# Attention, then two MoE layers: U = v_m w_in formed one head at a time in 64 by 32 tiles

## The chip, the cores and the metric

One core of a Trainium2 chip runs the whole program. The metric is the device time of one execution in microseconds (us); lower is better.

## The reference

Three layers run one after the other. Attention over a small memory comes first: for each of 8 batches and 8 heads, 576 rows of `k` and `v` are gathered into 32 memory rows.

```python
a   = softmax(phi, axis=2)                      # b h s m, m = 32
k_m = einsum('bhsm,bhsd->bhmd', a, k)           # normalised by the sum over m
v_m = einsum('bhsm,bhsd->bhmd', a, v)           # 32 x 64 for each batch and head
attn = softmax(q @ k_m.T / 8)                   # b h s m
x = (attn @ v_m) laid out as 4608 x 512
x = relu(x @ w_in) ** 2 @ w_out                 # 512 -> 2048 -> 512
logits = x @ w_gate; e = argmax(logits)         # 8 experts, each 512 -> 1024 -> 512
out = gate * relu(x @ w1[e]) @ w2[e]
```

The inputs come in double precision; the kernel reads them as pairs of 32-bit words.

## The kernel before

The kernel never forms `attn @ v_m`. It folds `v_m` into `w_in`: for each batch b, `U = v_m w_in` has one row for each (head, memory row), 256 rows, and 2048 columns, and the hidden layer is `attn U`. The 8 heads are two groups g of four heads; the 128 rows of a group fill the 128 partitions of a bank.

Stage one makes tokens in 12 blocks of 384 (`NB`), and each block in 16 steps f (`NF`), n counting all 192 steps. `g1(n)` (L638) multiplies `attnT` with a slice of U (L650, six matmuls for each batch in the block), ScalarE squares the result (L658 to L661), VectorE takes the remainder (L662), and `g2` (L675, matmuls at L670) accumulates the second layer. Between these steps the main loop puts in pieces of three generators: `attention(b)` for the next batch, `weight_stream()` (L577), which loads the experts' weights, splits them in two halves of 16 bits and stores them, and `route()` (L711) for finished blocks. Stage two, from about 840 us on, runs the experts over 39 tiles (`e1_mm`, `e2_mm`). In stage one a planner, which runs when the kernel is built, fixes the order of the instructions on each engine out of the program's order, priorities and dependencies.

Inside `attention(b)`, `s_kv` makes `k_m` and `v_m` in four column tiles of 32 (L366) and writes each head's 64 columns twice, next to each other, into `kvn` (L385). `s_tr(g)` (L390) transposes them, so that the 64 dimensions lie in partitions 0 to 63 and again in 64 to 127. A `mask` (L399) then zeroes, in each pair of heads, the half that belongs to the other head; the result is `vbd`. `s_scale` (L402) splits `vbd` into two halves of 16 bits, `v16`, for batches from `UB` = 3 on. `u_steps(b)` (L539) makes U: for each of four chunks of 512 columns (ch) and each g, one bank of `side_bank` (L95, three banks, shared with every other small product) is filled by two column tiles of 64 (x), each a matmul with all 128 rows, half of which multiply zeros. Batches 0 to 2 do that in fp32 (L554; every fp32 matmul runs as two instructions), batches 3 to 7 in three fp16 products (L563). ScalarE then writes the high half of U (L569) and VectorE the low half (L570). Each (ch, g) is one step of the generator; the loop takes one to three steps for each n.

`w_in` is loaded in 16 jobs of 128 rows by `load_next` (L208, DMA at L215) on SyncE's queue, through a ring of four places (`RAWS`). Job n holds rows `128 (n % 4)` on, that is two heads, and chunk `n // 4`. `conv` (L224) turns each into fp32. The 16 jobs of `w_out` follow through the same ring.

## Time and profile before

| | |
|---|---|
| median of 3 runs | 1335.16 us (1334.47 to 1335.77) |
| the profiled execution | 1334.69 us |
| its span, first to last instruction | 1332.6 us |
| TensorE matmul busy | 1173.5 us, 88% |
| VectorE, ScalarE busy | 676.7 us, 661.2 us |
| mean granted clock of TensorE | 0.958 of 2.4 GHz |

PE is TensorE's matmul, PEld its weight load, DVE VectorE, ACT ScalarE, SP SyncE with its queue of DMAs. The PE's busy time is the union of its matmuls' times from start to modelled end; two matmuls that follow each other overlap by the length of the array's pipeline, so the distance from start to start says more than one duration. U shows up under the tile name `u` (the bank) and `U` (the result).

### The profile page before, as it was taken

Reading aid. Unit: us, or ns where it says so; the run is one execution under the profiler, and the core shown is the slowest. Engines: PE = TensorE matmul, PEld = TensorE weight load, DVE = VectorE, ACT = ScalarE, POOL = GpSimd, SP = SyncE. Lnnn points to the kernel's source line nnn. Section 1 sums busy time; section 2 is a strip of 40 time slices with the busy share of each in tenths; the row PEclk is TensorE's granted clock in tenths of the full one; section 3 lists DMA queues with packets and bytes.
Section 4 is the critical chain, followed back from the end, with each engine's and each line's share of the span. In section 5 each row is a group of like instructions: output and inputs, shape, how many; then the busy total and the mean of one; then the engine's idle time right before and its main releaser. Section 6 shows DMA issues by size and latency. Waiting matters only on the chain.

```text
span 1332.6 us, 21300 instructions
## 1 busy us (share of the span) xinstructions
PE 1173.5 (88%) x7146; PEld 597.4 (45%) x7146; DVE 676.7 (51%) x1644; ACT 661.2 (50%) x1347; POOL 113.9 (9%) x169
## 2 busy tenths in 40 slices
PE   1538989998988998898999999998998998879896
PEld 1214546444545544455555465543443443334342
DVE  5798987877886885786546543342110111101100
ACT  2467877797875877685666665521111111111111
POOL 2000000101010101000000100013000000000000
PEclk9558999998989999898999999999999999999998
DMA  6957659468749469536040110476558457695762
GB/s 168 261 190 207 189 137 265 158 213 260 216 163 266 154 213 287 159 132 150 24 103 10 40 25 24 126 169 167 97 120 181 104 123 193 151 227 118 151 159 61
DMA packets 264369, 205.23 MB, mean 154 GB/s; under 512 B 209855, under 2 KB 228287, under 8 KB 264256
## 3 DMA queue, kind: packets, MB, share of 16 engines
q1 hardware_dynamic: 257616, 182.67, 53.7%
q0 software_dynamic: 6640, 21.16, 4.6%
q8 instruction: 58, 0.95, 0.3%
q14 instruction: 55, 0.45, 0.1%
HBM read 234.53 MB, written 55.76 MB: 218 GB/s over the span
## 4 chain that ended last, share of the span: by engine, by line
issue 33%; PE 24%; DMA 17%; DVE 13%; ACT 6%; POOL 4%; SPq 2%; POOLq 0%; ACTq 0%; DVEq 0%
PE acc L670 12%; DMA wstage<-in_moe_w_dram 6%; PE h L650 6%; POOL out_dram L92 3%; DMA scr<-rec,sl 2%; DMA e_t<-in_phi_dram 2%; DVE wo L629 2%; ACT wo L628 1%; DMA ws<-wo 1%; PE u L563 1%; DMA raw_ring<-in_moe_w_out_dram 1%; DVE g L662 1%; DMA raw_ring<-in_moe_w_in_dram 1%; ACT wo L601 1%; DVE wm L180 1%
## 5 line engine op out<-in xcount | busy, mean ns | idle before, releaser
L670 PE MATMUL acc<-wo,g 128*128 128x512 f16 x1728 | 421.1, 383 | 16.5 <-DVE g L662 9.9
L670 PEld LDWEIGHTS <-g 128*128 128x128 f16 x1728 | 166.0, 99 | 197.5 <-issue 22.1
L650 PE MATMUL h<-attnT,U 128*128 128x384 f16 (+1 forms) x1536 | 233.5, 290 | 13.8 <-ACT U L569 9.8
L1001 PE MATMUL e<-w2t,gT 128*128 128x512 f16 x936 | 211.5, 381 | 22.3 <-DMA gT<-g 14.6
L974 PE MATMUL e<-w1t,xT 128*128 128x512 f16 x936 | 211.2, 381 | 11.4 <-DMA w1t<-ws 8.0
L986 DVE SCALAR_TENSOR_TENSOR g<-e,g 128x512 f16<-128x512 f32 x78 | 50.3, 686 | 297.5 <-ACT g L985 297.3
L650 PEld LDWEIGHTS <-U 128*128 128x128 f16 x1536 | 140.1, 99 | 104.2 <-issue 26.6
L1001 PEld LDWEIGHTS <-gT 128*128 128x128 f16 x936 | 91.2, 98 | 137.4 <-DMA gT<-g 18.5
L974 PEld LDWEIGHTS <-xT 128*128 128x128 f16 x936 | 91.5, 98 | 124.9 <-issue 13.7
L662 DVE TENSOR_TENSOR g<-r,g 128x384 f16<-128x384 f32 x192 | 105.6, 553 | 78.3 <-ACT r L661 77.8
L658 ACT ACTIVATE r<-h 128x384 f32<-128x384 f32 x192 | 92.6, 485 | 80.7 <-PE h L650 58.7
L985 ACT ACTIVATE g<-e 128x512 f16<-128x512 f32 x78 | 42.3, 594 | 173.6 <-PE e L974 173.6
L1014 ACT ACTIVATE y<-e,fac 128x512 f32<-128x512 f32 x39 | 26.8, 688 | 197.9 <-PE e L1001 190.8
L660 ACT ACTIVATE g<-r 128x384 f16<-128x384 f32 x192 | 99.6, 522 | 8.8 <-PE acc L670 5.2
L661 ACT ACTIVATE r<-r 128x384 f32<-128x384 f32 x192 | 99.5, 521 | 3.9
L629 DVE SCALAR_TENSOR_TENSOR wo<-wstage,wsc,wo 128x1024 f16<-128x1024 f32 x64 | 81.1, 1280 | 21.7 <-ACT wo L628 21.6
L628 ACT ACTIVATE wo<-wstage,wsc 128x1024 f16<-128x1024 f32 x64 | 71.7, 1144 | 25.0 <-DMA ws<-wo 12.6
L92 POOL DMA_INDIRECT out_dram<-y,rt x39 | 37.9, 972 | 377.1 <-ACT y L1014 356.5
L92 POOL DMA_INDIRECT scr<-rec,sl x36 | 37.6, 1043 | 301.8 <-DVE sl L788 66.7
L366 PE MATMUL kvm<-kv,e_t 128*32 128x128 f32 x768 | 28.0, 302 | 28.4 <-ACT e_t L348 27.4
L180 DVE TENSOR_REDUCE wm<-wstage 128x1 f32<-128x1024 f32 x32 | 38.8, 1214 | 14.4 <-DMA wstage<-in_moe_w_dram 14.3
L601 ACT ACTIVATE wo<-wstage 128x1024 bf16<-128x1024 f32 x32 | 33.7, 1054 | 12.3 <-DMA wstage<-in_moe_w_dram 11.0
(240 smaller groups left out, 1088.2 us busy)
## 6 DMA issues: line engine op xcount, KB each, us to landing
w1t<-ws SPq DMA_DIRECT2D x144, 512.0 KB
w2t<-ws SPq DMA_DIRECT2D x144, 512.0 KB
wstage<-in_moe_w_dram SPq DMA_DIRECT2D x64, 512.0 KB
ws<-wo SPq DMA_DIRECT2D x64, 512.0 KB
kv<-in_k_dram SPq DMA_DIRECT2D x16, 576.0 KB
kv<-in_v_dram SPq DMA_DIRECT2D x16, 576.0 KB
q<-in_q_dram SPq DMA_DIRECT2D x64, 144.0 KB
raw_ring<-in_moe_w_in_dram SPq DMA_DIRECT2D x16, 512.0 KB
```

Source lines behind the costliest of these rows:

```text
L92: i = G.indirect_dma_start(out=dst[:, :], out_offset=bass.IndirectOffsetOnAxis(ap=index, axis=0), in_=src, in_offset=None, bounds_check=bo ...
L180: V.tensor_reduce(dst, src, axis=AX.X, op=ALU.max, apply_absolute_value=True)
L628: A.activation(hi, src, AF.Copy, scale=s)
L629: V.scalar_tensor_tensor(lo, src, s, hi, ALU.mult, ALU.subtract)
L650: T.matmul(bank[:, off:off + w], u_t[b][:, g, uh, f * P:(f + 1) * P], attnT[b][:, g, ah, s0:s0 + w], start=(x == 0), stop=(x == len(seq) - 1),
L658: A.activation(r, bank[:, 0:BLK], AF.Relu, scale=2.0 ** -10)
L660: A.activation(g[:, 0], r, AF.Square)
L661: A.activation(r, r, AF.Square)
L662: V.tensor_tensor(g[:, 1], r, g[:, 0], op=ALU.subtract)
L670: T.matmul(a, g[:, gh, tt * P:(tt + 1) * P], wo[:, f, wh, :], start=(f == 0 and x == 0), stop=(f == NF - 1 and x == 2),)
L974: T.matmul(bank[hf], x[:, 4 * xh + c, :].bitcast(F16), w[c][:, wh * F + hf * 512:wh * F + (hf + 1) * 512], start=(c == 0 and xh == 0 and w ...
L1001: T.matmul(a, gT[:, 8 * gh + f, :], w[f // 2][:, o:o + DM], start=(f == 0 and x == 0), stop=(f == 7 and x == 2),)
```

## The change

It touches three places. In `load_next`, the eight `w_in` jobs of the second group (n % 4 of 2 or 3) are loaded as two DMAs of 64 rows that swap the upper and the lower half of the partitions. In `s_tr`, the product with the mask becomes a plain copy, so `vbd` holds each head's values in both halves. In `u_steps`, one step takes a whole chunk: it takes two banks, one for each g, and issues for each product eight matmuls of 64 rows by 32 columns, one for each head; the half in which a head's rows lie alternates, so that the eight occupy eight different tiles of the array. The evictions of bank 0 stand in the same step, those of bank 1 in the next. The number of steps, of evictions and of streamed columns for each matmul stays.

```diff
-        SP.dma_start(raw, src)
+        if job[0] == "in" and job[1] % 4 >= 2:
+            SP.dma_start(raw[0:64], src[64:128])
+            SP.dma_start(raw[64:128], src[0:64])
+        else:
+            SP.dma_start(raw, src)
...
-            V.tensor_tensor(vbd[:, g, :], bank[:, P:2 * P], mask, op=ALU.mult)
+            V.tensor_copy(vbd[:, g, :], bank[:, P:2 * P])
...
         for ch in chunks:
+            if ch != chunks[0]:
+                yield
+            cs = slice(ch * 512, (ch + 1) * 512)
+            bank = [side_bank(f"u{b}_{ch}_{g}") for g in range(2)]
+            for i, (vh, wh) in enumerate(((0, 0),) if b < UB else ((0, 0), (0, 1), (1, 0))):
+                for hh in range(4):
+                    for g in range(2):
+                        r = slice(64 * ((hh + g) % 2), 64 * ((hh + g) % 2) + 64)
+                        m = slice(32 * hh, 32 * hh + 32)
+                        n = 4 * ch + 2 * g + hh // 2
+                        if b < UB:
+                            T.matmul(
+                                bank[g][m, :], vbd_t[b][r, g, m], w_in_sb[r, n + 1],
+                                start=True, stop=True,
+                            )
+                        else:
+                            T.matmul(
+                                bank[g][m, :], v16_t[b][0][r, vh, g * P + 32 * hh:g * P + 32 * hh + 32],
+                                w_in_16[r, n, wh], start=(i == 0), stop=(i == 2),
+                            )
             for g in range(2):
-                if not first:
+                if g == 1:
                     yield
...
-                A.activation(u[:, g, 0, cs], bank, AF.Copy, scale=sc)
+                A.activation(u[:, g, 0, cs], bank[g], AF.Copy, scale=sc)
                 V.scalar_tensor_tensor(
-                    u[:, g, 1, cs], bank, sc, u[:, g, 0, cs], ALU.mult, ALU.subtract
+                    u[:, g, 1, cs], bank[g], sc, u[:, g, 0, cs], ALU.mult, ALU.subtract
                 )
```

## Rows read from the trace of the kernel before

**Rows 1.** The page, part 1: busy time, share of the span, instructions.

```profile
PE 1173.5 (88%) x7146; PEld 597.4 (45%) x7146; DVE 676.7 (51%) x1644; ACT 661.2 (50%) x1347; POOL 113.9 (9%) x169
```

**Rows 2.** Busy time by stretch: length, PE, PEld, DVE, ACT, POOL; PEclk, DMA share, GB/s.

```profile
0.00:104.00 104.00, 36.45 (x204) 17.33 (x204) 78.23 (x166) 46.49 (x93) 10.30 (x55) 0.70 0.77 207
140.00:300.00 160.00, 151.63 (x1038) 80.07 (x1036) 132.36 (x270) 127.93 (x247) 9.23 (x11) 0.99 0.64 191
300.00:640.00 340.00, 307.27 (x2219) 172.82 (x2219) 255.44 (x624) 246.81 (x515) 30.31 (x35) 0.95 0.67 196
640.00:770.00 130.00, 130.00 (x876) 68.38 (x874) 69.25 (x199) 80.47 (x175) 8.20 (x9) 1.00 0.18 43
```

**Rows 3.** Who PE waited for from 104 to 770 us: total, times, longest.

```profile
PE acc L670 <- DVE g L662: 9.9, 9, 3.1
...
PE u L563 <- DVE U L570: 1.4, 1, 1.4
PE u L554 <- DVE U L570: 0.9, 1, 0.9
```

**Rows 4.** Busy time of all instructions in the windows of U, batches 1 to 5.

```profile
173.00:191.00 18.00, 14.59 (x79) 5.96 (x78) 15.07 (x34) 15.90 (x29) 0.35 (x1) 0.91 0.43 133
263.00:288.00 25.00, 25.00 (x119) 9.55 (x118) 18.23 (x29) 23.63 (x44) 0.35 (x1) 1.00 0.66 201
373.00:396.00 23.00, 19.19 (x177) 10.13 (x178) 18.05 (x54) 18.56 (x38) 2.05 (x3) 0.85 0.55 191
467.00:487.00 20.00, 18.52 (x112) 8.64 (x111) 15.87 (x21) 16.20 (x30) 0.00 (x0) 1.00 0.87 251
575.00:594.00 19.00, 19.00 (x167) 10.40 (x169) 16.76 (x42) 16.82 (x36) 0.00 (x0) 1.00 0.28 111
```

**Rows 5.** Likewise, instructions on tile u alone (PE, PEld, DVE, ACT), batches 2, 5, 7.

```profile
263.00:288.00 25.00, 8.41 (x32) 1.67 (x32) 4.48 (x6) 4.08 (x6) 1.00 0.66 201
...
575.00:594.00 19.00, 6.13 (x48) 0.00 (x0) 4.96 (x7) 4.46 (x8) 1.00 0.28 111
...
740.00:760.00 20.00, 6.33 (x48) 0.00 (x0) 5.16 (x7) 4.97 (x8) 1.00 0.00 1
```

**Rows 6.** PE's timeline at one fp32 group of U: start us, us, instructions.

```profile
286.86 1.08 PE L554 MATMUL u<-w_in_sb,vbd 128*64 128x512 f32 x4
287.87 2.12 PE L670 MATMUL acc<-wo,g 128*128 128x512 f16 x9
```

**Rows 7.** PE's timeline: matmuls of g2, one fp16 group of U, three groups together.

```profile
374.21 4.05 PE L670 MATMUL acc<-wo,g 128*128 128x512 f16 x18
378.19 0.84 PE L563 MATMUL u<-w_in_sb,v 128*64 128x512 f16 x6
...
586.35 2.13 PE L563 MATMUL u<-w_in_sb,v 128*64 128x512 f16 x18
```

**Rows 8.** PE's timeline: matmuls of s_kv in four column tiles of 32.

```profile
290.50 1.30 PE L366 MATMUL kvm<-kv,e_t 128*32 128x128 f32 x40
```

**Rows 9.** Groups by line: evictions of U, the product with the mask, a plain copy.

```profile
L570 DVE SCALAR_TENSOR_TENSOR U<-u,vts,U 128x512 f16<-128x512 f32 x40 | 29.1, 745 | 10.8 <-ACT U L569 10.6
L569 ACT ACTIVATE U<-u,vts 128x512 f16<-128x512 f32 x40 | 26.3, 682 | 11.5 <-PE u L563 11.5
L706 DVE COPY x2f<-acc 128x512 f32<-128x512 f32 x12 | 8.2, 683 | 2.6 <-PE acc L670 2.6
L399 DVE TENSOR_TENSOR vbd<-kvT,mask 128x128 f32<-128x128 f32 x16 | 4.5, 281 | 0.0
```

**Rows 10.** SyncE's timeline: one load's issue, and the last two loads of w_in.

```profile
41.04 0.33 SPq L215 DMA_DIRECT2D raw_ring<-in_moe_w_in_dram  x1
...
61.15 4.65 SPq L215 DMA_DIRECT2D raw_ring<-in_moe_w_in_dram  x2
```

**Rows 11.** SyncE's queue, waits up to 110 us: total, times, longest.

```profile
SPq L215 <- DVE w_in_sb L237: 35.2, 12, 6.9
SPq L215 <- DVE wo L237: 24.7, 11, 4.6
```

## What the change was predicted to do, and why

> **What bounds the kernel now.** I began with the busy times of the page: TensorE 88% of the span, VectorE and ScalarE about half [rows 1]. A share over the whole span mixes stages, so the next view is busy time by stretch [rows 2]. Up to 104 us PE works 36.45 of 104 us and VectorE 78.23: the start waits for loads and conversions. From 140 to 300 us PE is busy 151.63 of 160, from 300 to 640 us 307.27 of 340, and from 640 to 770 us 130.00 of 130. So PE sets the pace wherever U is made for batches 1 to 7, but not alone: from 300 to 640 us it stands still 32.7 us, while VectorE and ScalarE are at 75% and 73%. The view of waits says for what: mostly for the remainder g of VectorE (9.9 us in 9 waits), hardly ever, in U, for a bank that its evictions still hold (1.4 and 0.9 us, once each) [rows 3]. The third view is the same table for the windows in which U is made. In batches 2 and 5 PE has no idle time at all (25.00 of 25, 19.00 of 19) [rows 4], nor in batches 6 and 7, which lie in the full stretch of rows 2; batches 1, 3 and 4 leave 3.4, 3.8 and 1.5 us [rows 4]. A microsecond taken from PE is worth a microsecond in the former and part of one in the latter.
>
> **What U costs PE, and what it will cost.** Restricted to tile u, PE is busy 8.41 us in an fp32 batch (batch 2) and 6.13 and 6.33 us in fp16 batches (5 and 7) [rows 5]; batch 6 has as many matmuls. A single fp32 group of four instructions takes 1.08 us, its successor starting 1.01 us after it [rows 6]. A single fp16 group of six takes 0.84 us, and three in a row 2.13 us [rows 7], so that each further group adds (2.13 - 0.84) / 2 = 0.65 us: three rounds of 512 columns, since 18 full-array matmuls of 512 columns go from 374.21 to 378.19, 0.22 us each [rows 7]. The two column tiles of a group thus run side by side.
>
> After the change a chunk is 24 fp16 matmuls (16 fp32 instructions) in place of two groups of six (four). Streamed columns for each stay 512. If the eight tiles run side by side, a chunk takes as many rounds as one group does now, plus the delay from tile to tile.
>
> What the trace does not show is two row halves at work together, nor eight tiles. Nearest is `s_kv`, four column tiles of 32 in fp32: 40 matmuls in 1.30 us, ten rounds, (1.30 - 0.3) / 9 = 0.11 us each with 0.3 us for the last to end [rows 8]. That is a quarter of an fp32 round of 512 columns (1.01 / 2 = 0.50 us, the change of tiling in it) [rows 6]: four tiles cost no more than two, and eight instructions (four loads, four matmuls) fit into 0.11 us. Twenty-four loads and 24 matmuls at that pace are 0.66 us, just what the three rounds take, so issue does not become the bound. The bounds for a chunk are 0.84 us (row halves as free as column tiles) and 0.84 + 0.65 = 1.49 us (the halves take turns). I take 0.87 us, with 0.03 us as my estimate for six more tiles, because the row nearest to it shows tiles in parallel; in fp32 1.08 + 0.03 = 1.11 us.
> The Trainium skill prices this ("TensorE: Matmul & The Clock Gate", section "Measured speedup vs the span model"): tiles in rows and columns run together at about 4 ns for each further tile. By it a chunk would be 0.84 + 6 x 0.004 = 0.86 us, an estimate from that page; no run here shows row halves yet.
>
> For an fp32 batch that is 8.41 - 4 x 1.11 = 4.0 us less on PE, for an fp16 batch 6.2 - 4 x 0.87 = 2.7 us. Batches 2, 5, 6 and 7, where PE is full: 4.0 + 3 x 2.7 = 12.1 us, all of it on the path. Batches 1, 3 and 4: 4.0 + 2 x 2.7 = 9.4 us; PE has idle time there, so part of the gain only lengthens a wait. I choose half, 4.7 us. Batch 0 lies in the start, where PE is mostly idle: nothing, with up to 3 us as the far bound. What is gained by batch 5 (4.7 + 4.0 + 2.7 = 11.4 us) still has to pass stalls up to 640 us; PE idles 10% there, and VectorE and ScalarE, with as much work in less time, will be late more often. I take a fifth off, 2.3 us. That leaves 14.5 us.
>
> **Two banks at a time.** A chunk cannot begin before two of the three side banks are free; now a group needs one. Its wait stands at the head of PE's queue, with the L650 and L670 matmuls behind it, and ScalarE waiting for those. A bank comes free after ScalarE's 0.682 us and VectorE's 0.745 us [rows 9]. So a chunk waits between 0 and 1.43 us, 28 chunks in batches 1 to 7: 0 to 40 us. The order is planned with banks in view, and only two of 56 groups waited for U's own evictions so far [rows 3]; the evictions of a batch fill only some 5 of 19 us on each engine [rows 5]. I take 0.05 us a chunk, 1.4 us.
>
> **The loads of w_in.** Eight jobs become two DMAs each: eight more issues on SyncE's queue at 0.33 us [rows 10], some 3 us with their gaps. Behind them stand the other loads of the start (k, v, q, phi, and then w_out, through the same ring). But the queue spends 35.2 and 24.7 us waiting for VectorE to empty the ring [rows 11], which covers most issues; the bytes are the same. Bounds: -1 us (a half lands earlier and its neighbour is not held up) to 3 us; I take 1 us, since the queue's waits are nearest. If that cover were gone, it is 3 us, which moves everything after it.
>
> **The mask.** 16 products of 281 ns become 16 copies. A plain copy out of a bank takes 683 ns for 512 columns against 745 for the product with remainder [rows 9]; for 128 columns a few tens of ns, below 1 us in all, either sign. Zero. Scales, norms and evictions issue as before; moving the second group's matmuls one step earlier adds no instruction.
>
> **The sum.** 14.5 - 1.4 - 1.0 = 12.1 us. The profiled execution took 1334.69 us (1332.6 us of span and 2.1 us around it), so 1322.6; the median of the runs stands 0.47 us above it: 1323 us.
>
> **The rivals.**
> A, the work moves to the evictions. PE is relieved, but ScalarE and VectorE, at 75% and in places more (23.63 of 25 us of ScalarE in batch 2 [rows 4]), now end last, and only batches 6 and 7, where they are at 53% to 62% [rows 2], give their 2 x 2.7 us. For it: the idle PE from 300 to 640 us. Against it: PE has no idle time in the windows of batches 2 and 5. Time: 1335.2 - 5.4 + 1.4 + 1.0 = 1332 us. The Trainium skill warns of this ("TensorEngine Tiling (Array Packing)", section "PSUM Bottleneck"): tiles speed up TensorE but not the emptying of PSUM; the 128 evictions of U do stay as they are.
> B, the change does not do what it says: the row halves take turns. A batch then costs 4 x 1.49 = 6.0 us against 6.1 to 6.3, about 0.3 us less, 2 us over seven batches, which the banks and the loads eat (2.4 us): 1335 to 1336 us. For it: no row shows row halves together. Against it: column tiles do run so.
> C, slower: the pair of banks stalls PE. It decides when the mean wait of the 28 chunks passes (14.5 - 1.0) / 28 = 0.48 us, a third of the 1.43 us that one bank's emptying takes. At 0.75 us it costs 21 us: 1335.2 - 13.5 + 21 = 1343 us; at the full 1.43 us 1362 us. For it: three banks for everything small, the routing included. Against it: [rows 3].
>
> **How the numbers follow.** My forecast has a chance of 0.62 (1311 to 1330 us on its own), A 0.15, B 0.08, C 0.15. A measurement of this kernel can tell about 0.2%, 2.7 us, from no change: A falls to the faster side with 0.09 and within with 0.06; B within with 0.07, slower with 0.01; C is slower. So faster 0.71, within 0.13, slower 0.16. The range begins where all of PE's 21.5 us and batch 0's 3 us arrive (1335 - 25 = 1310) and ends with C's middle, 1343; some 0.05 lies below and 0.08 above.
>
> **What would show it.** Right, step by step: in PE's timeline 24 fp16 matmuls of U that take about 0.87 us and 16 fp32 ones about 1.11 us (B: 1.5 us and 2.1 us); PE busy on tile u near 3.5 us in an fp16 batch; the stretch 640 to 770 us still full but shorter, the second stage from 840 us on unchanged in length; PE's waits for VectorE's U still near 2 us (C: over 13 us); PE's idle time from 300 to 640 us near 37 us (A: 41 us, all of batches 3 to 5's 8.1 us added); the last load of w_in issued within 3 us of 65.8 us [rows 10]. Wrong would make it above all a different order: the planner lays out every queue anew, and a shift of a load, or of a batch's softmax ahead of g, can move several us in either direction that no row of before can price.

## The result, and the profile after

The changed kernel takes 1350.1 us (median of 4 runs, 1349.63 to 1350.26), the kernel before 1334.82 us beside it: ratio 1.0117, 95% interval [1.0101, 1.0133]. It is slower. The profiled execution took 1350.26 us, its span is 1348.6 us: 15.6 and 16.0 us more than before.

Page part 1 of the kernel after, which answers to [rows 1]: PE's busy time is 1.3 us less, and the span 16.0 us more.

```profile
PE 1172.2 (87%) x7482; PEld 593.7 (44%) x7482; DVE 680.2 (50%) x1644; ACT 658.7 (49%) x1347; POOL 113.6 (8%) x169
```

Busy time by stretch of the kernel after, which answers to [rows 2] (length, PE, PEld, DVE, ACT, POOL, PEclk, DMA share, GB/s):

```profile
140.00:300.00 160.00, 140.76 (x966) 73.41 (x965) 124.72 (x262) 119.46 (x234) 9.52 (x13) 0.95 0.65 187
300.00:640.00 340.00, 304.59 (x2406) 169.61 (x2405) 256.04 (x610) 246.53 (x513) 28.35 (x33) 0.97 0.71 201
640.00:770.00 130.00, 128.53 (x1011) 70.91 (x1011) 78.29 (x225) 84.67 (x189) 7.53 (x8) 0.99 0.20 42
```

From 140 to 300 us PE works 10.9 us less than before, at a lower granted clock (0.95 against 0.99), and VectorE and ScalarE work 7.6 and 8.5 us less: the whole core is behind there. In the next two PE's busy time differs by 2.7 and 1.5 us.

The same by progress. A hidden step n is taken to begin with ScalarE's first instruction on it (L658 before, L664 after; read from the timelines). The table gives its start, after minus before, in us:

| n | 0 | 8 | 16 | 24 | 40 | 72 | 112 | 128 | 144 | 191 | end of span |
|---|---|---|---|---|---|---|---|---|---|---|---|
| before | 110.2 | 144.1 | 185.6 | 214.0 | 280.6 | 421.9 | 584.3 | 651.8 | 715.8 | 866.2 | 1332.6 |
| after minus before | +3.8 | +2.6 | +12.8 | +18.8 | +19.4 | +12.9 | +19.0 | +17.4 | +13.2 | +13.1 | +16.0 |

So the loss has three places. 3.8 us are lost before the first step, 15.0 us between steps 0 and 24, that is while batch 1's attention is made (step 16 is the first that needs its U), and 2.9 us in stage two, which took 463 to 473 us in all twenty kernels told of here, so that this is no finding. Between 24 and 128 the kernel gains 1.4 us, and from 128 to 191, where batches 6 and 7 are made, 4.3 us.

**U on PE.** PE's timeline of the kernel after, which answers to [rows 6, 7]: first the fp32 batch 2, then fp16 chunks of batches 3 and 6.

```profile
290.87 1.09 PE L563 MATMUL u<-w_in_sb,vbd 64*32 64x512 f32 x16
...
300.95 1.06 PE L563 MATMUL u<-w_in_sb,vbd 64*32 64x512 f32 x8
...
303.02 1.06 PE L563 MATMUL u<-w_in_sb,vbd 64*32 64x512 f32 x8
...
401.13 0.82 PE L568 MATMUL u<-w_in_sb,v 64*32 64x512 f16 x11
...
402.00 0.39 PE L568 MATMUL u<-w_in_sb,v 64*32 64x512 f16 x1
...
402.58 0.83 PE L568 MATMUL u<-w_in_sb,v 64*32 64x512 f16 x12
...
682.81 0.85 PE L568 MATMUL u<-w_in_sb,v 64*32 64x512 f16 x24
...
687.47 1.48 PE L568 MATMUL u<-w_in_sb,v 64*32 64x512 f16 x36
```

Where a chunk's two banks stand next to each other, eight tiles work at once: 24 fp16 matmuls in 0.85 us, 16 fp32 instructions in 1.09 us. But most chunks don't stand so. At 300.95 and 303.02 the two banks of one chunk come 2 us apart, eight instructions each, and each takes as long as a group took before (1.06 against 1.08 us); at 401.13 and 402.58 an fp16 chunk comes as 12 and 12. At 687.47 one and a half chunks make 1.48 us. Nothing but the program's order holds the 24 together, and the planner may place each matmul by itself; that it does so where a bank comes free is likely, and not shown. Tile u of the kernel after, in the windows of batches 2, 5, 6 and 7, which answers to [rows 5]:

```profile
279.00:304.00 25.00, 7.38 (x64) 1.10 (x64) 4.39 (x6) 4.00 (x6) 1.00 0.82 239
...
596.00:606.00 10.00, 5.43 (x96) 0.00 (x0) 3.66 (x6) 3.88 (x6) 1.00 0.01 2
682.00:697.00 15.00, 3.80 (x96) 0.00 (x0) 4.48 (x7) 4.83 (x8) 1.00 0.40 54
753.00:772.00 19.00, 6.39 (x96) 0.00 (x0) 5.07 (x7) 5.15 (x8) 1.00 0.00 1
```

Only batch 6 has nearly all its chunks whole, 3.80 us; batch 7 costs what it cost before (6.39 against 6.33 us). Over batches 1 to 7 the union of U's matmuls falls from 51.1 to 44.6 us, by 6.5 us.

**PE's waits** from 104 to 770 us of the kernel after, which answers to [rows 3] (total, times, longest):

```profile
PE acc L676 <- DVE g L668: 9.7, 9, 5.2
PE h L656 <- ACT U L575: 7.6, 2, 6.8
PE h L656 <- ACT r L664: 6.2, 5, 2.2
PE kvT L399 <- ACT qT L445: 5.4, 1, 5.4
PE kvm L371 <- DMA kv<-in_v_dram: 5.4, 3, 2.6
PE kvm L371 <- DVE U L576: 4.2, 3, 3.0
...
PE u L563 <- DVE U L576: 2.5, 3, 1.9
PE u L568 <- DVE U L576: 2.0, 3, 1.1
```

U's own waits for its banks are 4.5 us (2.3 before), and the next batch's k and v product now waits 4.2 us for a bank that U holds.

**The early loss.** VectorE's timeline around batch 1's second k_m, v_m (L385 before, L390 after), first of the kernel before:

```profile
119.35 0.48 DVE L385 TENSOR_SCALAR kvn<-kvm,rs 128x256 f32<-128x256 f32 x1
...
126.31 0.48 DVE L385 TENSOR_SCALAR kvn<-kvm,rs 128x256 f32<-128x256 f32 x1
...
128.53 1.22 DVE L180 TENSOR_REDUCE wm<-wstage 128x1 f32<-128x1024 f32 x1 [0.97 <-DMA wstage<-in_moe_w_dram]
```

And of the kernel after:

```profile
124.45 0.47 DVE L390 TENSOR_SCALAR kvn<-kvm,rs 128x256 f32<-128x256 f32 x1
...
132.77 1.22 DVE L180 TENSOR_REDUCE wm<-wstage 128x1 f32<-128x1024 f32 x1 [4.02 <-DMA wstage<-in_moe_w_dram]
...
139.93 0.47 DVE L390 TENSOR_SCALAR kvn<-kvm,rs 128x256 f32<-128x256 f32 x1
```

Before, the second kvn comes first and the weight stream's reduction (L180) behind it. After, the order is the other way round: VectorE stands 4.02 us for the stream's DMA, works on the stream, and the second kvn begins 13.6 us later than before. Everything of batch 1 that hangs on it follows. VectorE's order is only part of these 13.6 us: the second product of k and v, which kvn needs, is late itself. On PE's timeline of the kernel before it ends at 125.47 us, after (last row of the second fence below) at 131.84 us. So 6.4 us lie in the product and 7.2 us in VectorE's queue behind it.

```profile
123.95 1.52 PE L366 MATMUL kvm<-kv,e_t 128*32 128x128 f32 x48
```

PE's timeline of the kernel after shows that its queue is another one too: the first product of k and v (L371, 48 instructions in one piece before) is cut by transposes of q that wait for a bank of U.

```profile
119.06 1.06 PE L371 MATMUL kvm<-kv,e_t 128*32 128x128 f32 x26
120.70 0.30 PE L440 MATMUL qTp<-ident,q 96*128 96x96 f32 x1 [0.58 <-DVE U L576]
...
122.06 0.84 PE L371 MATMUL kvm<-kv,e_t 128*32 128x128 f32 x18
...
130.32 1.52 PE L371 MATMUL kvm<-kv,e_t 128*32 128x128 f32 x48 [0.26 <-DMA kv<-in_v_dram]
```

The buffer of k and v is read until 122.9 us, and SyncE's queue issues the next load only then (before at 115.62 us). The last load of `w_in`, now two halves, had been issued at 73.45 us, 7.6 us later than before (65.80 us, [rows 10]). SyncE's timeline of the kernel after, both:

```profile
72.34 0.47 SPq L217 DMA_DIRECT2D raw_ring<-in_moe_w_in_dram  x1
72.86 0.59 SPq L218 DMA_DIRECT2D raw_ring<-in_moe_w_in_dram  x1
...
122.94 0.33 SPq L324 DMA_DIRECT2D kv<-in_k_dram  x1
```

### The profile page after: what moved, and what is told of

It reads as the page before. It is cut to its first block, busy times and chain, and to the rows that moved or that the text cites. A ratio compares the mean times of both kernels' runs of the same rounds, so it can differ in the third digit from the quotient of the medians.

```text
span 1348.6 us, 21987 instructions
## 1 busy us (share of the span) xinstructions
PE 1172.2 (87%) x7482; PEld 593.7 (44%) x7482; DVE 680.2 (50%) x1644; ACT 658.7 (49%) x1347; POOL 113.6 (8%) x169
## 4 chain that ended last, share of the span: by engine, by line
issue 35%; PE 26%; DMA 18%; DVE 10%; ACT 5%; POOL 4%; SPq 1%; POOLq 0%; ACTq 0%; DVEq 0%
PE acc L676 14%; PE h L656 7%; DMA e_t<-in_phi_dram 4%; DMA wstage<-in_moe_w_dram 4%; POOL out_dram L92 3%; DMA kv<-in_v_dram 2%; DMA ws<-wo 2%; DVE wo L635 2%; PE kvm L371 1%; DMA scr<-rec,sl 1%; DMA raw_ring<-in_moe_w_in_dram 1%; DMA raw_ring<-in_moe_w_out_dram 1%; DVE mx L341 1%; ACT wo L634 1%; PE u L568 1%
## 5 line engine op out<-in xcount | busy, mean ns | idle before, releaser
L676 PE MATMUL acc<-wo,g 128*128 128x512 f16 x1728 | 419.4, 383 | 11.9 <-DVE g L668 9.7
L1007 PE MATMUL e<-w2t,gT 128*128 128x512 f16 x936 | 215.0, 386 | 21.7 <-DMA gT<-g 15.2
L980 PE MATMUL e<-w1t,xT 128*128 128x512 f16 x936 | 209.8, 379 | 12.8 <-DMA w1t<-ws 10.2
L664 ACT ACTIVATE r<-h 128x384 f32<-128x384 f32 x192 | 92.2, 484 | 71.9 <-PE h L656 57.9
L371 PE MATMUL kvm<-kv,e_t 128*32 128x128 f32 x768 | 30.7, 310 | 37.5 <-ACT e_t L353 27.2
L180 DVE TENSOR_REDUCE wm<-wstage 128x1 f32<-128x1024 f32 x32 | 38.8, 1213 | 15.9 <-DMA wstage<-in_moe_w_dram 15.8
L1018 DVE TENSOR_TENSOR fac<-rt,vals 128x1 f32<-128x1 f32 x35 | 5.5, 157 | 77.0 <-DMA rt<-scr 77.0
```

The costliest lines, as they stand in the source:

```text
L664: A.activation(r, bank[:, 0:BLK], AF.Relu, scale=2.0 ** -10)
L676: T.matmul(a, g[:, gh, tt * P:(tt + 1) * P], wo[:, f, wh, :], start=(f == 0 and x == 0), stop=(f == NF - 1 and x == 2),)
L980: T.matmul(bank[hf], x[:, 4 * xh + c, :].bitcast(F16), w[c][:, wh * F + hf * 512:wh * F + (hf + 1) * 512], start=(c == 0 and xh == 0 and w ...
L1007: T.matmul(a, gT[:, 8 * gh + f, :], w[f // 2][:, o:o + DM], start=(f == 0 and x == 0), stop=(f == 7 and x == 2),)
```

## The experiments

All in one table: the ratio to the kernel before, timed beside it; the starts of four hidden steps in the profiled run, minus those of the kernel before, in us; and PE's time on U in batches 1 to 7 (51.1 us before). In the column "batch 0", 64 means tiles of 64 by 32 there, 128 the old ones. "Whole" means that no load of `w_in` is cut. The starts and PE's time are those of one execution of each kernel, which lies up to 5.9 us above the median of its runs (i2_after_exchanged, 1351.15 against 1345.29 us) and up to 4.9 us below it (g4_whole_loads, 1345.47 against 1350.36 us), so that starts which differ by a few us are not told apart.

| kernel | loads | batch 0 | ratio, 95% interval | n 0 | n 24 | n 128 | n 191 | U on PE |
|---|---|---|---|---|---|---|---|---|
| after | cut | 64 | 1.0117 [1.0101, 1.0133] | +3.8 | +18.8 | +17.4 | +13.1 | 44.6 |
| e1_split_loads | cut | 128 | 1.0075 [1.0048, 1.0103] | +3.1 | +4.2 | +6.2 | +6.3 | 50.1 |
| e2_pair_step | whole | 128 | 0.9947 [0.9914, 0.9980] | -1.8 | -0.8 | -6.5 | -7.2 | 53.8 |
| e3_same_tiles | whole | 64 | 1.0115 [1.0089, 1.0141] | +0.1 | +20.5 | +13.6 | +12.1 | 51.7 |
| e4_together | cut | 64 | 1.0107 [1.0070, 1.0143] | +3.2 | +16.3 | +18.3 | +13.4 | 38.1 |
| f1_batch0_old | whole | 128 | 1.0027 [0.9994, 1.0059] | -0.4 | +6.1 | +5.8 | +4.0 | 56.2 |
| f2_fp16_four | whole | 128 | 0.9987 [0.9960, 1.0014] | -1.4 | -2.3 | -3.2 | -3.7 | 53.7 |
| f3_eight_fp16 | whole | 128 | 1.0061 [1.0031, 1.0091] | -3.3 | +1.9 | +9.7 | +4.0 | 41.2 |
| f4_exchanged | whole | 128 | 1.0012 [0.9983, 1.0040] | -0.7 | -1.7 | -2.3 | -1.7 | 49.7 |
| g1_eight_last | whole | 128 | 0.9933 [0.9909, 0.9956] | +0.0 | -0.0 | -7.2 | -11.9 | 47.3 |
| g2_after_b0_old | cut | 128 | 1.0115 [1.0087, 1.0144] | +1.5 | +3.1 | +11.8 | +8.7 | 44.2 |
| g3_q_behind_kv | cut | 64 | 1.0029 [1.0006, 1.0052] | +3.9 | +20.3 | +4.7 | +0.5 | 44.5 |
| g4_whole_loads | whole | 64 | 1.0146 [1.0125, 1.0168] | +0.5 | +21.9 | +16.4 | +11.8 | 42.6 |
| h1_eight_untied | whole | 128 | 1.0002 [0.9981, 1.0023] | -3.0 | +1.2 | -2.0 | -6.5 | 45.6 |
| h2_four_tied | whole | 128 | 1.0094 [1.0060, 1.0128] | -2.9 | -1.6 | +8.6 | +9.5 | 54.5 |
| h3_eight_from5 | whole | 128 | 0.9928 [0.9903, 0.9953] | -2.6 | -0.5 | -9.0 | -14.8 | 44.9 |
| i1_whole_b0_old | whole | 128 | 1.0068 [1.0044, 1.0093] | -1.2 | +0.4 | +8.2 | +5.3 | 44.5 |
| i2_after_exchanged | cut | 64 | 1.0068 [1.0039, 1.0097] | +5.3 | +17.6 | +14.0 | +9.8 | 45.7 |
| i3_after_g1_first | cut | 64 | 1.0107 [1.0077, 1.0136] | +3.9 | +21.0 | +17.5 | +13.2 | 46.9 |

### The parts one by one

**e1_split_loads**: the kernel before, with the eight loads of the second group cut into two, not exchanged.

```diff
-        SP.dma_start(raw, src)
+        if job[0] == "in" and job[1] % 4 >= 2:
+            SP.dma_start(raw[0:64], src[0:64])
+            SP.dma_start(raw[64:128], src[64:128])
+        else:
+            SP.dma_start(raw, src)
```

> The kernel before, with the eight w_in loads of the second group each cut into two DMAs of 64 rows, not swapped; nothing else. Theory L (the loads cost the start): the first hidden step begins about 4 us later, as in the changed kernel (114.0 against 110.2 us), and the end with it, 1338 to 1340 us. Rival N (the loads are hidden, the late start comes from the new order of everything else): first step within 1 us of 110.2 us and 1334 to 1337 us in all.

Step 0 starts 3.1 us later, and the kernel is slower by 0.75%. The five other kernels with cut loads and 64 by 32 tiles in batch 0 start step 0 at +3.2 to +5.3 us, g2 at +1.5 us, those with whole loads at -3.3 to +0.5 us. The cut costs some 3 us at the start, by itself. But step 40 of e1 begins 0.3 us before that of the kernel before, and step 56 7.5 us after: the 0.75% are not these 3 us carried to the end.

**e2_pair_step**: the kernel before with the changed step structure alone: two banks for each step, tiles of 128 by 64, mask and loads as before.

```diff
-                bank = side_bank(f"u{b}_{ch}_{g}")
+            bank = [side_bank(f"u{b}_{ch}_{g}") for g in range(2)]
...
+            for g in range(2):
+                if g == 1:
+                    yield
```

> The kernel before with the changed kernel's steps alone: a step takes both banks of a chunk and issues the 128 by 64 matmuls of both groups, loads and mask as before. Theory B (two banks at a time disturb the plan): slower by 6 us or more, above all between 144 and 214 us, where the changed kernel loses 15 us. Rival T (the tiles themselves do it: twice the matmuls to plan): within 3 us of 1335 us.

0.9947: the pair of banks costs nothing; with the matmuls free to be placed one by one, the kernel is a little faster, which neither theory said, by about as much as an edit without any work can move a kernel (see below).

**e3_same_tiles**: the changed kernel with whole loads, without the exchange of halves; both groups use the same four tiles, so that the two row halves of one strip of columns never work at once.

```diff
-                        r = slice(64 * ((hh + g) % 2), 64 * ((hh + g) % 2) + 64)
+                        r = slice(64 * (hh % 2), 64 * (hh % 2) + 64)
```

> The changed kernel with whole w_in loads and without the swap: both groups then use the same four 64 by 32 tiles, so no two matmuls of different row halves share a column strip. If row halves working together are worth what PE's time on tile u shows in the changed kernel (6.5 us less than before in batches 1 to 7), PE's time on u rises back to 51 us or more here. Theory L gives 4 us less at the first step than the changed kernel, about 1346 to 1352 us in all; if the order alone makes the loss, anything between 1335 and 1352 us.

PE spends 51.7 us on U, as before the change, and the ratio is that of the changed kernel. Its neighbour with whole loads and eight tiles, g4_whole_loads, spends 42.6 us there and comes to 1.0146. So what eight tiles save there doesn't show at the end, and what costs 1.2% is there without cut loads and without eight tiles.

**e4_together**: the changed kernel with a chunk's matmuls tied to their order, one behind the other, the second group's first.

```diff
-                    for g in range(2):
+                    for g in (1, 0):
...
+                        with tc.issue_after(one.ins) if one is not None else ExitStack():
```

> The changed kernel with each chunk's matmuls tied in their order, so that PE's queue holds the two banks' matmuls alternating and together. Theory S (the plan pulls the two banks' matmuls apart, four tiles work at a time, and the gain stays away): a chunk of 24 takes about 0.8 us, PE's time on u in an fp16 batch falls from 5.4 us to 3.4 us, and the kernel gains some 10 to 15 us on the changed one: 1335 to 1341 us. Rival H (row halves don't run together): a chunk of 24 takes about 1.4 us and the time stays at 1350 us or rises, as each chunk now waits for two banks.

PE's time on U falls to 38.1 us, 13.0 us below the kernel before, and an fp16 batch costs 3.9 to 5.1 us. PE's timeline of e4_together, two pieces of batch 7 (a chunk's first matmul can run ahead of the other 23: that of the first row ran alone at 759.60 us):

```profile
763.53 0.84 PE L570 MATMUL u<-w_in_sb,v 64*32 64x512 f16 x23
...
775.86 0.84 PE L570 MATMUL u<-w_in_sb,v 64*32 64x512 f16 x24
```

But the time is the same as without the tie (1.0107): the gain reaches PE and not the end. Whether the tie itself eats it, this pair doesn't say (see f3 and h1 below).

### Batch 0

**f1_batch0_old**: e3_same_tiles with batch 0 back in tiles of 128 by 64. The product with the mask is back too, in every batch.

```diff
-            V.tensor_copy(vbd[:, g, :], bank[:, P:2 * P])
+            V.tensor_tensor(vbd[:, g, :], bank[:, P:2 * P], mask, op=ALU.mult)
...
+            if b == 0:
+                for i, (vh, wh) in enumerate(prods):
...
+                        for x in range(2):
+                            if b < UB:
+                                T.matmul(
+                                    bank[g][64 * x:64 * x + 64, :],
+                                    vbd_t[b][:, g, 64 * x:64 * x + 64],
+                                    w_in_sb[:, 4 * ch + 2 * g + x + 1],
+                                    start=True, stop=True,
+                                )
```

> e3_same_tiles (1348 us) with batch 0 alone back in 128 by 64 matmuls, in the same pair step, mask kept. Theory Q (the tiles of batch 0 put U's matmuls ahead of batch 1's first k, v product in PE's queue, and from there batch 1 runs 10 to 15 us late): hidden step 16 begins within 4 us of the kernel before (185.6 us; 198.9 in e3_same_tiles), and the end falls to 1326 to 1338 us. Rival T (64 by 32 tiles cost wherever they stand): step 16 stays above 192 us and the end near 1345 us.

Step 24 comes 14.4 us earlier than in e3, step 191 8.1 us; the ratio falls by 0.9%.

**g2_after_b0_old**: the changed kernel with the same edit of the matmuls, the mask back for batch 0 alone, in two views of it.

```diff
-            V.tensor_copy(vbd[:, g, :], bank[:, P:2 * P])
+            if b == 0:
+                mw = mask[:, 32 * g:32 * g + 64].unsqueeze(1).to_broadcast([P, 2, 64])
...
+            else:
+                V.tensor_copy(vbd[:, g, :], bank[:, P:2 * P])
```

> The changed kernel with batch 0 alone back in 128 by 64 matmuls (its mask with the halves of the second group exchanged, as the loads exchange them). Theory Q: hidden step 16 at 188 to 190 us instead of 198.4 us (the loads' 3 us stay), and 9 to 12 us less than the changed kernel at the end, 1337 to 1342 us. Rival: the later batches lose it in any case, 1345 to 1351 us.

Step 24 comes 15.7 us earlier, but step 128 only 5.6 us and step 191 4.4 us, and the ratio is unchanged.

**g4_whole_loads**: the changed kernel with whole loads. In place of the halves of `w_in`, the heads of the second group are exchanged in pairs, from the k and v product on; with that go four small matmuls for a sum in place of one, and another view of the mask.

```diff
-                        e_t[:, 4 * g + hh, j, :],
-                        t[:, :, hh, j, :],
+                        e_t[:, 4 * g + (hh ^ g), j, :],
+                        t[:, :, hh ^ g, j, :],
...
-            SP.dma_start(raw[0:64], src[64:128])
-            SP.dma_start(raw[64:128], src[0:64])
```

> The changed kernel with the second group's heads exchanged in pairs from the k, v product on, in place of the exchanged halves of w_in, so that every w_in load is one DMA again; the eight tiles as in the changed kernel. Theory L: first hidden step at 110 us instead of 114, and 3 to 8 us less at the end, 1342 to 1347 us. Rival N: within 2 us of the changed kernel, 1348 to 1352 us.

Step 0 comes 3.3 us earlier than in the changed kernel, and nothing of it is left at step 24; the ratio, 1.0146, is no lower.

**i1_whole_b0_old**: g4_whole_loads with batch 0 in the old tiles.

```diff
-                V.tensor_copy(vbd[:, g, :], bank[:, P:2 * P])
+            if b == 0:
+                V.tensor_tensor(
+                    vbd[:, g, :].rearrange("p (a n) -> p a n", a=2),
+                    bank[:, P:2 * P].rearrange("p (a n) -> p a n", a=2), mk, op=ALU.mult,
+                )
+            else:
+                V.tensor_copy(vbd[:, g, :], bank[:, P:2 * P])
...
+            if b == 0:
+                for i, (vh, wh) in enumerate(prods):
...
+                        for x in range(2):
```

> The changed kernel with two of its parts undone together: loads whole (heads of group 2 exchanged from s_kv on instead) and batch 0 in 128 by 64 tiles with its mask; batches 1 to 7 in eight tiles, untied. Each part undone alone gave nothing (g2_after_b0_old 1.0115, g4_whole_loads 1.0146). Theory: either of the two late starts is enough to lose the same time, so undoing both brings back 12 to 16 us: ratio 0.999 to 1.004, hidden step 0 to 128 in 540 to 546 us. Rival: the loss is made by the tiles of batches 1 to 7 whatever the start: ratio stays at 1.010 or more and the stretch above 550 us.

Step 24 comes 21.5 us earlier than in g4, step 191 6.5 us, and the ratio is 0.8% lower: between what the two theories said. Its stretch from step 0 to 128, 551.0 us, is the rival's.

What goes along with batch 0's tiles, and with their mask, which these edits put back together, is the same in every kernel. VectorE's timeline of g4_whole_loads (64 by 32):

```profile
121.24 0.48 DVE L392 TENSOR_SCALAR kvn<-kvm,rs 128x256 f32<-128x256 f32 x1
...
131.75 1.22 DVE L180 TENSOR_REDUCE wm<-wstage 128x1 f32<-128x1024 f32 x1 [3.62 <-DMA wstage<-in_moe_w_dram]
...
137.78 0.47 DVE L392 TENSOR_SCALAR kvn<-kvm,rs 128x256 f32<-128x256 f32 x1
```

And that of i1_whole_b0_old, which differs from it in batch 0 alone:

```profile
118.20 0.47 DVE L392 TENSOR_SCALAR kvn<-kvm,rs 128x256 f32<-128x256 f32 x1
...
125.17 0.48 DVE L392 TENSOR_SCALAR kvn<-kvm,rs 128x256 f32<-128x256 f32 x1
...
128.08 1.22 DVE L180 TENSOR_REDUCE wm<-wstage 128x1 f32<-128x1024 f32 x1 [1.67 <-DMA wstage<-in_moe_w_dram]
```

In the seven kernels with 64 by 32 tiles in batch 0 the weight stream stands ahead of batch 1's second kvn on VectorE, kvn starts at 133.5 to 141.5 us, and step 24 is 16.3 to 21.9 us late. In the kernel before and all twelve others kvn stands first, at 123.0 to 128.5 us, and step 24 is -2.3 to +6.1 us off. The second product of k and v divides them the same way: it ends at 129.9 to 133.5 us in the seven and at 122.3 to 127.7 us in the rest. That is shown. Why the planner turns the two around when batch 0's matmuls change is not: batch 0's U costs PE nearly the same (11.97 us before, 11.52 after).

**g3_q_behind_kv**: the changed kernel with batch 1's first transposes of q queued behind the product of k and v on PE.

```diff
-                    T.transpose(
...
+                    with tc.issue_after(kv_last[0].ins) if b == 1 and pr == 0 else ExitStack():
+                        T.transpose(
```

> The changed kernel with one order forced: in batch 1 the first transposes of q stand behind the k, v product in PE's queue, not between its matmuls. Theory Q1 (that product's end, 3.5 us late for a bank that U holds, delays the next load of k and v, and all of batch 1 with it): the product ends near 121 us instead of 123.0, the next load of k follows it, and step 16 comes 3 us or more earlier than 198.4 us. Rival Q2 (the second product stands late in PE's queue whatever the load does): step 16 within 2 us of 198.4 us, 1347 to 1351 us.

The k and v product runs in one piece again (48 instructions from 119.45 us), step 16 comes 3.7 us earlier; but step 24 is as late as before the edit (+20.3 us), since VectorE's order stayed, kvn at 137.4 us. The 0.9% that this kernel gains on the changed one come after step 24, where the edit touches nothing: another order. The cut product is thus not what makes step 24 late. Nor does a late step 24 fix the end: this kernel wins 19.8 us back from there to step 191 (+0.5 us), while g2 is only 3.1 us late at step 24 and ends at 1.0115.

### Eight tiles in the later batches

**f2_fp16_four** and **f3_eight_fp16**: e2_pair_step with 64 by 32 tiles in batches 3 to 7 alone. f2 uses four tiles for both groups and isn't tied; f3 uses eight, with the exchanged heads of g4, and is tied as in e4. Of f3:

```diff
+                for i, (vh, wh) in enumerate(prods):
+                    for hh in range(4):
+                        for g in (1, 0):
+                            half = (hh + g) % 2
...
+                            with tc.issue_after(one.ins) if one is not None else ExitStack():
```

> The pair step (1326 us as e2_pair_step) with 64 by 32 tiles in the fp16 batches 3 to 7 alone, both groups in the same four tiles, whole loads, mask kept. Theory Q: nothing is lost ahead of batch 3, and PE's time on u stays at 6 to 7 us a batch: 1322 to 1332 us. Rival T: 1335 to 1345 us.

> The pair step with eight tiles, tied together, in the fp16 batches 3 to 7; fp32 batches in 128 by 64. The four heads of the second group change places in pairs from the k, v product on, with a second view of the mask, so that the eight tiles differ without any swap in the loads of w_in, which stay whole. If the loads and batch 0 are the whole loss, PE spends 3.5 to 4.5 us a batch on u in batches 3 to 7 instead of 6 to 7, some 10 us less, and the kernel ends at 1312 to 1324 us, below e2_pair_step. If a freed PE is not what the end waits for, it ends within 4 us of e2_pair_step (1326 us).

f2 stays near the kernel before. f3, at 1340.8 us slower than either theory said, takes 9.9 us off PE's time on U and needs 13.1 us more from step 0 to 128 than the kernel before (554.7 against 541.6 us, in which PE stands still 58.9 us against 44.3), and 5.7 us less from 128 to 191.

**h1_eight_untied** and **h2_four_tied** cross the two: f3 without the tie, f2 with it; the tie goes with the second group first, as in e4. Of h1 (h2 is the reverse edit of f2):

```diff
-                        for g in (1, 0):
+                        for g in range(2):
...
-                            with tc.issue_after(one.ins) if one is not None else ExitStack():
```

> f3_eight_fp16 without the tie of a chunk's matmuls: the planner may place them one by one again, g=0 first. Three theories for why f3 needs 554.7 us from hidden step 0 to 128 where f2_fp16_four, the same step with four tiles, needs 539.9. Tie: a tied chunk holds PE's queue until both banks are free; then untied the stretch falls to within 3 us of 540, PE's time on u rises above 46 us (chunks torn apart) and the kernel comes to 0.997 to 1.000. Speed: chunks that take half the time bring their evictions in a bunch; then the stretch follows PE's time on u: near 540 if chunks are torn, near 553 if not. Exchange: the exchanged heads of group 2 (four small matmuls for a sum in place of one, another mask) cost it; then the stretch stays above 550 and the ratio near 1.006 whatever PE's time on u.

> f2_fp16_four with the tie: heads not exchanged, both groups on the same four tiles, so nothing of PE's time on u is saved (a chunk near 1.5 us, u near 53 us). Tie: hidden step 0 to 128 takes 550 us or more and the ratio is 1.004 to 1.008, as in f3. Speed or exchange: the stretch stays within 3 us of f2's 539.9 and the ratio within 0.997 to 1.001.

From step 0 to 128 f2 needs 539.9 us, h1 542.6, h2 553.1, f3 554.7. In these two pairs the tie costs 12 to 13 us there, with four tiles as with eight; neither the eight tiles nor the exchange of heads does. In a third pair it doesn't: the changed kernel needs 555.3 us there, e4 with its tie 556.7 us. By the ratio f3 lies 0.6% above h1 and h2 1.1% above f2; the first is hardly more than an edit without any work can do (see below). Busy time from 300 to 640 us of h1 (no tie; length, PE, PEld, DVE, ACT, POOL, PEclk, DMA share, GB/s):

```profile
300.00:640.00 340.00, 308.92 (x2422) 174.32 (x2420) 258.66 (x635) 246.87 (x519) 30.34 (x36) 0.96 0.70 200
```

The same stretch of h2 (tie):

```profile
300.00:640.00 340.00, 300.22 (x2308) 168.98 (x2309) 248.61 (x594) 238.99 (x497) 27.44 (x33) 0.96 0.69 196
```

All three engines get less done in the same time. Part of it is seen at the banks. PE's waits of f3, from 104 to 790 us, for the matmuls of U that wait for U's evictions (total, times, longest):

```profile
PE u L600 <- DVE U L608: 6.0, 5, 4.2
```

The same of h1:

```profile
PE u L600 <- DVE U L608: 2.1, 6, 0.8
```

In h2 that wait is 1.4 us, however, so that the rest, if it isn't chance, lies with the work that was planned around the tied chunks.

**g1_eight_last** and **h3_eight_from5**: e2_pair_step with eight tied tiles from batch 6 and from batch 5 on.

```diff
+UE = 6
...
+            if b < UE:
...
+            else:
+                one = None
```

> e2_pair_step with the eight tied tiles in batches 6 and 7 alone, where PE is full; the heads' places change in those two batches only, loads whole. Theory F (where PE is full the tiles give their predicted 2.7 us a batch): PE spends about 4 us instead of 6 on u in each, the stretch from hidden step 128 to 191 takes 208 to 209 us instead of 213.6, and the kernel ends some 4 to 5 us below e2_pair_step, 1319 to 1324 us. Rival C (two banks at a time stall PE wherever they are taken): no gain or a loss on e2_pair_step, 1325 us or more.

> g1_eight_last with the eight tied tiles from batch 5 on instead of 6. Batch 5's U is made where PE still waits at times. If a freed microsecond of PE pays wherever PE is full at that point, some 2 us more than g1: ratio 0.991 to 0.993. If only the last two batches pay and the tie costs before them, it falls back to 0.995 to 1.000.

From step 128 to 191 the kernel before needs 214.4 us, e2 213.7, g1 209.7, h3 208.6: here 12.5 us of PE on U become 8.1, and PE has no idle time. Busy time from 640 to 770 us of h3:

```profile
640.00:770.00 130.00, 130.00 (x1014) 69.19 (x1013) 72.95 (x214) 84.89 (x184) 7.24 (x8) 1.00 0.16 40
```

The stretch from step 128 to 191 separates all kernels: the twelve with eight tiles in batches 6 and 7 gain 2.9 to 5.8 us in it, whether tied or not, the seven others between 1.8 us and -0.9 us. The untied eight of the twelve save 2.3 us of PE on U there and gain 2.9 to 4.6 us, so that the shorter matmuls are not all of it; what the rest is stays open. g1 and h3 are faster than both kernels, 0.9933 and 0.9928; whether they beat e2 (0.9947) their intervals don't say.

### The planner's own spread

**f4_exchanged**, **i2_after_exchanged** and **i3_after_g1_first** change no work. f4 exchanges two neighbouring lines of VectorE in the kernel before, i2 the same two in the changed kernel, i3 takes the second group first in each pair of matmuls. The edit of i2:

```diff
+            V.tensor_copy(vbd[:, g, :], bank[:, P:2 * P])
             V.tensor_tensor(kb, bank[:, 0:P], mask, op=ALU.mult)
-            V.tensor_copy(vbd[:, g, :], bank[:, P:2 * P])
```

> The kernel before with two VectorE instructions exchanged (the product that makes vbd ahead of the one that makes kb), the same work. It measures what a new plan alone does to the time. Theory Q needs a small effect here, within 3 us of the kernel before; if it moves by 6 us or more, differences of that size between the other kernels can be the plan's chance.

> The changed kernel with its two VectorE lines for kb and vbd exchanged, which changes no work, only the planner's input, as f4_exchanged does for the kernel before (1.0012). If the loss belongs to the change, it stays: 1.009 to 1.014. If it is one unlucky order among many, it moves by 0.4% or more, in either direction.

> The changed kernel with the bank of group 2 first in each pair of matmuls, untied: the same work, another input for the planner. If the loss belongs to the change: 1.009 to 1.014, and PE's time on u stays near 45 us, since chunks are torn as before. If the order of the pair decides whether a chunk is torn: u near 40 us. If the loss is one unlucky order among many, the ratio moves by 0.4% or more.

1.0012, 1.0068 and 1.0107: an edit without any work moved the changed kernel by half a per cent. The three samples of the same work (the changed kernel, i2 and i3) are 0.7 to 1.2% slower than the kernel before, and all have the late kvn. That is no lower end of what the change costs: g3, which only forces an order upon it, comes to 1.0029. How much of the 1.2% belongs to the change and how much to the order that it was given is open. The spread also says what single pairs are worth: 0.66% from h1 to i1 (eight tiles in batches 1 and 2, lost between steps 56 and 112) is hardly more than such luck, and no mechanism for it was found.

## Why the prediction was wrong

Forecast were 1323 us and a range up to 1343; measured 1350. Two steps failed. From the price of a chunk the sum went to all chunks of seven batches, 21.5 us of PE's time, of which 6.5 us came, and 4.3 us at the end of stage one. And batch 0, with the order of the start, was put at nothing, where 15.0 us were lost. Of the span's 16.0 us, 18.8 are lost by step 24, 1.4 and 4.3 won back, 2.9 added in stage two.

**The price of a chunk was right.** 0.87 and 1.11 us were forecast, 0.85 and 1.09 us stand in the trace where a chunk is whole. Row halves do work side by side; rival B falls. By the Trainium skill ("TensorE: Matmul & The Clock Gate", section "Measured speedup vs the span model") 0.86 us was the estimate; the 0.85 us of this trace agree.

**The number of whole chunks was wrong: the step from a chunk's price to a batch's.** 8.41 - 4 x 1.11 and 6.2 - 4 x 0.87 took for granted that a chunk's matmuls stay together. Most came in two halves, each at the price of a group before. 21.5 us of PE's time became 6.5 (13.0 when tied). The text had both facts, two banks for a chunk and an order that is planned with banks in view, and didn't join them.

**Where PE is full, the gain arrived; before that, it didn't.** 5.4 us were forecast for batches 6 and 7; whole chunks give 4.7 to 5.8 us there (e4, f3, g1, h3), the changed kernel 4.3. Batches 2 and 5 were counted as full too, since their windows of 25 and 19 us had no idle PE [rows 4]. A window that follows the work is not a stretch: what it gives back can go into the next wait. h3, with eight tiles in batch 5 too, needs as long as g1 from step 0 to 128 (535.2 against 534.4 us). That only batches 6 and 7 pay is what rival A said, and its 5.4 us are nearer than the forecast's 14.5. Its reason, that ScalarE and VectorE now end last, is not shown: from 300 to 640 us PE stands still 35.4 us, 2.7 us more than before, while U costs it 3.5 us less in batches 3 to 5, so that most of this saving seems to have become a wait, but no row says that evictions make it. The Trainium skill ("TensorEngine Tiling (Array Packing)", section "PSUM Bottleneck") warns that tiles don't speed up the emptying of PSUM; no run here isolates that emptying.

**Rival C** did not come about in the changed kernel: U waits 4.5 us for its banks, where C named over 13 us. Untied, the pair of banks costs nothing (e2); tied, it cost 12 to 13 us in two pairs (h1 and f3, f2 and h2) and 1.4 us in the third (the changed kernel and e4). That the changed kernel escapes the wait by tearing the chunk, which would be the loss of the gain in another form, fits the rows and is not shown.

**The loads were mis-sized**: 1.0 us was taken, 3 us the bound; 3.1 us in e1 and 3.8 us in the changed kernel were measured. The price was one issue at 0.33 us more for each job. The last job's two halves take 0.47 and 0.59 us in place of 0.33, all eight jobs 10.2 us in place of 5.9 on SyncE's timeline, and the queue's waits did not cover it: the last load was issued 7.6 us later. How much of it reaches the end is open, since e1 is level again at step 40 and g4, without the cut, is no faster than the changed kernel.

**The mask** is nothing, as forecast: 0.28 us for the product and 0.28 us for the copy (VectorE's timelines at 123.16 us before, 126.24 us after).

**Batch 0 was put at nothing, and there the largest loss lies.** "Batch 0 lies in the start, where PE is mostly idle: nothing, with up to 3 us as the far bound", and that bound was a gain. For PE that is so. But batch 0's U stands beside the first weight stream and batch 1's k and v in the queues, and with other matmuls there the planner laid out PE's and VectorE's queues so that batch 1 came 14 us later: 15.0 us from step 0 to 24, more than the whole sum. The last paragraph of the prediction named such an order and gave it neither a price nor a chance. A rough size was to be had from the trace of before: the second kvn hangs 7 us behind the first, with the weight stream's reductions, which wait for a DMA, next in the queue; a swap costs the stream's whole piece. This says where the time went in the profiled run, not that batch 0 alone decides the end: g2, without the late start, ends at 1.0115, and g3, as late as the changed kernel at step 24, at 1.0029.

**Left open.** What makes the whole slower by 1.2% and not merely no faster; how much of it is the order that this one plan happened to get; why the planner turns those two around; why the gain of batch 0's old tiles reaches the end in two pairs (e3 and f1, g4 and i1: 8.1 and 6.5 us of 14.4 and 21.5) and not in the third (after and g2); what batches 1 and 2 lose.

## What to carry to other kernels

In this kernel a saving reached the end only where the bounding engine had no idle time over a long stretch. Try such an edit there alone first (batches 6 and 7 here) and leave every earlier batch's instructions as they were. A gain that needs instructions side by side needs something that keeps them so, and that tie can have its own price; try tie and tiles apart, as h1 and h2 do. Before believing a difference of half a per cent, plan both kernels again with an edit that changes no work.

## What the runs showed of the hardware

- Eight tiles of 64 by 32 cost 0.02 to 0.03 us more than four: 1.09 us for 16 fp32 instructions against 1.06 for 8, 0.85 for 24 fp16 matmuls against 0.82 to 0.83 for 11 or 12.
- Four tiles of 64 by 32 cost what two of 128 by 64 did: 1.06 against 1.08 us in fp32 [rows 6], 0.83 against 0.84 us in fp16 [rows 7].
- The last load of `w_in`, cut into two of 64 rows, holds SyncE's queue for 0.47 and 0.59 us; a whole one held it for 0.33 us [rows 10].
